# The sequence transform of an FNet layer as seven products of block sums, with an accumulating DMA

## The chip, the cores and the metric

One Trainium2 chip, one NeuronCore. The metric is the device time of one execution in microseconds (us), the median of the runs shown. PE is the matmul engine, DVE the vector engine, ACT the scalar engine, POOL is GpSimd, and SP is the engine whose queue issues nearly all DMAs here.

## The reference

Two independent halves, each 2048 x 1024, end up side by side in one output of 2048 x 2048 in float32.

```python
# left half: sliding-window attention, 32 heads of 32, window 256
q, k, v = split_heads(x @ wqkv)
scores  = where(0 <= i - j < 256, (q @ k.T) * 32 ** -0.5, -1e9)
a       = concat_heads(softmax(scores) @ v) @ wo
# right half: FNet mixing, only the real part
re = x @ dft_hid_re.T;  im = x @ dft_hid_im.T            # "first spectral product"
y  = dft_seq_re @ re - dft_seq_im @ im                   # "second spectral product", 2048 x 2048 by 2048 x 1024
out = concatenate([a, y], axis=-1)
```

## The kernel before

Every float32 operand is scaled by a power of two found from its own largest value, and split into a high and a low float16 part; a product is three matmul passes (high x high, high x low, low x high: `PASSES`). One matmul is 128 x 128 weights by 128 x 512 moving columns.

The program runs in this order on PE. First the projections q, k and v (`order`, 96 products of 24 matmuls). Then the spectral half, `units`: for each part p (0 is the real part, 1 the imaginary part) 16 units "x" and then 16 units "c". An x unit i multiplies the 128 rows i of x by the hidden DFT matrix, two column halves e of 24 matmuls each, and ACT and DVE write the result as a high and a low half into `ain` (a view of the large tile `reg1`). A c unit i multiplies 128 rows of the cosine (or sine) matrix by all 16 row blocks in `ain`: two halves e of 48 matmuls each. For p = 0 ACT copies each half from PSUM into a tile `y` (line 764), which goes to a DRAM scratch `y1s`; for p = 1 `y` is loaded back from there, DVE adds the new product (line 766), and `y` goes to `out`. Last comes the output projection "po" of the attention (line 792), which already works with seven products of block sums instead of eight blocks.

The rows of a unit are fetched two units ahead (`u_load`), scaled and split one unit ahead (`u_split`; the splits run in `split`, lines 109 to 112, ACT writing the high part and DVE the low part; on the page DVE's part has line 106). For a c unit the largest absolute value of its 128 x 2048 rows is found by two DVE reductions (`u_top`, tile `top_u`), spread over the partitions by a PE transpose, and turned into a scale (`scale_of`).

The attention is a generator (`attention`) of 256 blocks, cut into two steps each. `tick` pulls `rate` steps for each matmul of the main work, so the blocks are spread evenly under the projections and the spectral half; it must be done before the last c units (`LAST`), where `wo_blocks` prepares the weights of the output projection. One block is: scores on PE (line 212), a masked copy, a maximum and a bias on DVE (220, 222, 225), two exponentials and a float16 copy on ACT (228, 231), the low part on DVE (232), a DMA transpose, two mask selections on POOL (245, 247), and the weighted sum of v on PE (274), closed by three small DVE operations (280, 282, 285) per two blocks and a split of `o` per eight blocks (294, 295).

The order of instructions on each engine is not that of the code: the framework's scheduler sets it at build time from its own estimates. Each engine then runs its queue strictly in that order and waits at the head of it. PSUM holds three banks for the main products (`ps_m`, tags m0 to m2, used in turn through `bank`), two pairs of banks for the scores, and one for the sums of v.

## Time and profile before

| | us |
|---|---|
| median of 3 runs | 1841.79 (1839.05 to 1841.85) |
| the profiled execution's own time | 1839.44 |
| its span, first to last instruction | 1837.7 |
| projections, up to the first x unit | 571 |
| x units, p = 0 and p = 1 | 571 to 764, 1133 to 1328 |
| c units, p = 0 and p = 1 | 764 to 1133, 1328 to 1686 |
| output projection | 1686 to 1837 |

The page gives each engine's busy time; the stage bounds above are the first and last starts of the groups of each stage. The granted PE clock is 0.997 over the span. A group's mean duration counts the overlap of neighbours: a matmul row of 379 ns follows its neighbour after less than that, so the pace of PE is read from runs of matmuls in the timeline, not from the mean.

### The profile page before, as it was taken

The numbers are of one execution on the slowest core, as the hardware profiler recorded it, in microseconds if no ns is written. First come the engines' busy times: TensorE is split into PE (matmuls) and PEld (weight loads), VectorE is DVE, ScalarE is ACT, GpSimd is POOL, SyncE is SP. The second block draws the span as 40 slices with busy tenths as digits, with TensorE's granted clock in tenths as the row PEclk, the third lists the DMA queues.
The fourth block names the chain that finished last, engine by engine and source line by source line (L and its number), as shares of the span: only waits on it lengthen the run. The fifth ranks groups of instructions, "written<-read, shape, count | busy, mean of one in ns | idle before, by whom it ended". The sixth has DMA issues, their size and how long they took to land.

```text
span 1837.7 us, 29866 instructions
## 1 busy us (share of the span) xinstructions
PE 1820.5 (99%) x11260; PEld 892.2 (49%) x11260; DVE 1233.2 (67%) x2444; ACT 755.1 (41%) x1207; POOL 327.5 (18%) x489
## 2 busy tenths in 40 slices
PE   7999999999999999999999999999999999999998
PEld 3444455445544554555455544554554455444443
DVE  7665887786666665777776666666677676685451
ACT  3332443454444444454444444544443333332221
POOL 0000122212212221222122212221222122200000
PEclk9999999999999999999999999999999999999999
DMA  5357799997676655568776676665486666662331
GB/s 229 115 181 207 212 221 233 233 218 167 153 171 146 127 127 117 133 171 183 173 151 153 155 155 166 127 138 121 95 198 173 162 161 146 146 184 69 115 104 69
DMA packets 438288, 289.55 MB, mean 158 GB/s; under 512 B 338816, under 2 KB 396160, under 8 KB 438144
## 3 DMA queue, kind: packets, MB, share of 16 engines
q1 hardware_dynamic: 438144, 287.65, 63.5%
q8 instruction: 88, 1.44, 0.3%
q14 instruction: 56, 0.46, 0.1%
HBM read 155.32 MB, written 58.85 MB: 117 GB/s over the span
## 4 chain that ended last, share of the span: by engine, by line
PE 94%; DVE 3%; DMA 1%; ACT 1%; issue 1%; SPq 0%; ACTq 0%; DVEq 0%
PE p L338 51%; PE pk L338 9%; PE pv L338 9%; PE po L792 8%; PE pq L338 8%; PE s L212 4%; PE pv L274 4%; DVE reg L106 1%; DMA raw_x<-in_xa_dram 0%; DVE raw_wo L664 0%; ACT reg L111 0%; DVE top_x L106 0%; DMA raw_wd<-in_wd_dram 0%; DVE ext L106 0%; DVE un L106 0%
## 5 line engine op out<-in xcount | busy, mean ns | idle before, releaser
L338 PE MATMUL p<-reg,un 128*128 128x512 f16 x4608 | 1048.1, 379 | 1.1 <-DVE un L106 1.0
L338 PEld LDWEIGHTS <-un 128*128 128x128 f16 x4608 | 439.8, 97 | 492.7 <-DVE un L106 2.0
L228 ACT ACTIVATE s<-s,bias,esc 128x256 f32<-128x256 f32 (+1 forms) x512 | 268.6, 528 | 554.8 <-DVE bias L225 454.5
L245 POOL TENSOR_SCALAR_AFFINE_SELECT z<-t 128x512 f16<-128x512 f16 x224 | 158.6, 708 | 1041.2 <-DMA t<-hl 946.0
L232 DVE TENSOR_TENSOR hl<-s,hl 128x512 f16<-128x512 f32 (+1 forms) x256 | 170.7, 670 | 195.5 <-ACT hl L231 194.7
L338 PE MATMUL pq<-reg,wu_q 128*128 128x512 f16 x768 | 176.1, 385 | 6.7 <-ACT reg L111 4.3
L338 PE MATMUL pk<-reg,wu_k 128*128 128x512 f16 x768 | 174.4, 379 | 0.0
L338 PE MATMUL pv<-reg,reg 128*128 128x512 f16 x768 | 172.9, 379 | 0.0
L222 DVE TENSOR_REDUCE mx<-s 128x2 f32<-128x512 f32 (+1 forms) x256 | 170.5, 667 | 3.1
L247 POOL TENSOR_SCALAR_AFFINE_SELECT t<-t 128x512 f16<-128x512 f16 x224 | 163.9, 732 | 15.3
L231 ACT ACTIVATE hl<-s 128x512 f16<-128x512 f32 (+1 forms) x256 | 148.4, 584 | 6.7
L212 PE MATMUL s<-qk,qk 96*128 96x128 f16 (+2 forms) x704 | 147.8, 275 | 0.0
L220 DVE COPY_PREDICATED s<-upper,s 128x256 f32<-128x256 uint32 x224 | 94.4, 423 | 63.4 <-PE s L212 61.8
L338 PEld LDWEIGHTS <-wu_q 128*128 128x128 f16 x768 | 74.9, 99 | 95.9 <-issue 12.1
L338 PEld LDWEIGHTS <-reg 128*128 128x128 f16 x768 | 73.7, 98 | 83.8
L338 PEld LDWEIGHTS <-wu_k 128*128 128x128 f16 x768 | 73.6, 98 | 82.3
L106 DVE SCALAR_TENSOR_TENSOR un<-raw_u,sc_u,un 128x1024 f16<-128x1024 f32 x64 | 86.7, 1383 | 23.2 <-ACT un L111 22.9
L274 PE MATMUL pv<-vt,t 128*128 128x65 f16 x1984 | 99.3, 185 | 0.0
L212 PEld LDWEIGHTS <-qk 96*128 96x128 f16 x704 | 65.8, 98 | 66.9
L274 PEld LDWEIGHTS <-t 128*128 128x128 f16 x1984 | 89.2, 96 | 10.9 <-POOL t L247 0.3
L111 ACT ACTIVATE un<-raw_u,sc_u 128x1024 f16<-128x1024 f32 x64 | 69.9, 1140 | 46.5 <-DVE sc_u L106 46.5
L274 PE MATMUL pv<-vt,z 128*128 128x65 f16 (+1 forms) x896 | 88.4, 185 | 0.0
(138 smaller groups left out, 1472.3 us busy)
## 6 DMA issues: line engine op xcount, KB each, us to landing
raw_u<-in_cs_dram SPq DMA_DIRECT2D x64, 512.0 KB, 4.9
qk<-qs SPq DMA_DIRECT2D x192, 128.0 KB, 3.2
raw_u<-in_xb_dram SPq DMA_DIRECT2D x32, 512.0 KB, 4.0
vs<-yv SPq DMA_DIRECT2D x32, 260.0 KB, 2.8
vt<-vs SPq DMA_DIRECT2D x32, 260.0 KB, 3.9
raw_x<-in_xa_dram SPq DMA_DIRECT2D x16, 512.0 KB, 10.2
qs<-yq SPq DMA_DIRECT2D x32, 256.0 KB, 2.4
raw_scan<-in_xb_dram SPq DMA_DIRECT2D x16, 512.0 KB, 4.2
```

Of the source, the lines that this page charges most:

```text
L106: latest[:] = [f(*args, **kwargs)]
L212: nc.tensor.matmul(s[:, j, at:at + (k1 - k0) * P], q2s[g, sc][:, h, i * P:i * P + P], k2s[g, k0 // QB][:, h, k0 % QB * P:k0 % QB * P + (k1 ...
L220: nc.vector.copy_predicated(s[:, :, 2 * P:3 * P], upper2, s[:, :, :P] if nb == 3 else never2)
L222: nc.vector.tensor_reduce(mx, sv, axis=AX.X, op=ALU.max, negate=True)
L228: nc.scalar.activation(sv[:, h], sv[:, h], AF.Exp, bias=bias[:, h:h + 1], scale=es)
L231: nc.scalar.activation(hi, sv, AF.Copy)
L232: behind[:] = [nc.vector.tensor_tensor(lo, sv, hi, op=ALU.subtract)]
L245: nc.gpsimd.affine_select(out=z, in_=pk, compare_op=ALU.is_gt, fill=0.0, base=0, pattern=[[0, 4], [-1, P]], channel_multiplier=1)
L247: nc.gpsimd.affine_select(out=pk, in_=pk, compare_op=ALU.is_ge, fill=0.0, base=0, pattern=[[0, 4], [1, P]], channel_multiplier=-1)
L274: nc.tensor.matmul(pvt[:, r, j, lo:], weights(part, j, kb), vts[g, k // QB][:, k % QB, at + lo:at + VW], start=(m == 0), stop=(m == len(se ...
L338: nc.tensor.matmul(ps, lhs(hl, d), rhs(hr, d), start=(m == 0), stop=(m == 3 * n - 1))
L792: nc.tensor.matmul(ps, lhs[pos](hl, k), slot(pos)[:, hr, k], start=(m == 0 and fresh), stop=(m == 11), skip_group_check=True)
```

## The change

The second spectral product is cut into four rounds: for each part p, two halves c of the contraction (1024 of 2048 rows). A round is 8 x units and then 8 c units. The x units of a round go in the order 0, 4, 1, 5, 2, 6, 3, 7, so that after each pair the two blocks to be combined are there: ACT evacuates them in float32 to a tile `tb` (line 828), and `t_blocks` forms from each pair seven block sums, high and low, in `tsum` (in `reg1`, where `ain` was): four subtractions, on POOL for the first three pairs and on DVE for the last, and copies on ACT and DVE.

A c unit now covers two row tiles (256 output rows) and half the contraction. `u_split` scales its two raw tiles, forms four sums of blocks on POOL in place (lines 631 and 640, 128 x 512 each), and splits seven 128 x 512 blocks in the tiles un_a, un_b, un_c and a spare part of `reg1`. `seven` then runs seven products of 12 matmuls (positions 0, 3, 2, 1, 4, 5, 6) into three PSUM banks: positions 0, 2, 4 and 6 go one after the other into bank a, 1 and 5 into bank b, 3 into bank c. Two positions after the first go on accumulating in a bank that has been read in between, so the read must be over before the next product starts there. Bank a of one unit is bank b of the next. ACT copies positions 0, 2, 1 and 6 to `y`, DVE adds 3, 4 and 5 there (lines 857 and 855).

There are three `y` buffers, two for each unit: the first of a unit, finished by position 6, is the second of the next unit, first written by that unit's position 2 or 1. In the first round SP stores them plainly to `out`; in the other three POOL issues a DMA that adds them to `out` in DRAM (line 864, 48 transfers of 512 KB). `y1s` is gone, with its 16 stores and 16 loads.

Moved besides: the search for the scale of a c unit goes from DVE to ACT, which sums absolute values (line 606, 64 passes over 128 x 1024); the factor `fc`, the scaling of `o` by the softmax sums and the low part of `ohl` go from DVE to POOL; raw tiles are fetched three units ahead; `rate` rises from 0.0869 to 0.0922 steps for each matmul, and the last-but-one c unit of the last round is now where the attention must be done.

```diff
-            nc.vector.tensor_tensor(                       # scaling of o, 128 times
+            nc.gpsimd.tensor_tensor(
-            nc.vector.tensor_tensor(ohl[:, 1], o, ohl[:, 0], op=ALU.subtract)
+            nc.gpsimd.tensor_tensor(ohl[:, 1], o, ohl[:, 0], op=ALU.subtract)
...
-    MM_ATT = 24 * (len(order) - START) + 4 * NT * 24 + 4 * NT * 48
+    MM_ATT = 24 * (len(order) - START) + 4 * 8 * 48 + 4 * 8 * 84
...
     for p in range(2):
-        units += [("x", p, i) for i in range(NT)] + [("c", p, i) for i in range(NT)]
+        for c in range(2):
+            units += [("x", p, c, 4 * (i % 2) + i // 2) for i in range(8)] + [("c", p, c, q) for q in range(8)]
...
     def u_top(n):
-            for k in range(2):
-                top(f"u{n}", raws[n][k], k, 2)
+            for j in range(2):
+                with tc.issue_after(behind_act[0].ins) if behind_act else nullcontext():
+                    nc.scalar.activation(junk, raws[n][j].rearrange("p d t -> p (d t)"), AF.Abs,
+                                         scale=2.0 ** -10, accum_out=tops[key][:, j:j + 1])
...
     def u_split(n):
+        nc.gpsimd.tensor_scalar(fc[n], fa[:, p:p + 1], v[:, 0:1], None, op0=ALU.mult)
+        ua, uc, ub = (stp.tile([P, 2, ND, P], F16, tag="st", name=f"un{n}_{k}") for k in "acb")
+        split(ua[:, 0], ua[:, 1], r1, s)
+        split(ud[:, 0], ud[:, 1], r2[:, 4:], s)
+        gsub(r1[:, :4], r1[:, :4], r2[:, :4])
+        nc.gpsimd.tensor_tensor(r2[:, :4], r2[:, :4], r2[:, 4:], op=ALU.add)
+        gsub(r2[:, 4:], r2[:, 4:], r1[:, :4])
+        gsub(r1[:, 4:], r1[:, 4:], r2[:, 4:])
+        return [lambda: split(uc[:, 0], uc[:, 1], r2, s), lambda: split(ub[:, 0], ub[:, 1], r1, s)]
...
+    def t_blocks(k, a, b):
+        def fill(i, src):
+            hi = tsum[:, i:i + 2, 0, k]
+            nc.scalar.activation(hi, src, AF.Copy)
+            nc.vector.tensor_tensor(tsum[:, i:i + 2, 1, k], src, hi, op=ALU.subtract)
+        sub = gsub if k < 3 else (lambda o, x, y: nc.vector.tensor_tensor(o, x, y, op=ALU.subtract))
+        nc.scalar.activation(tsum[:, 0, 0, k], a[:, 0], AF.Copy)
+        nc.vector.tensor_tensor(tsum[:, 0, 1, k], a[:, 0], tsum[:, 0, 0, k], op=ALU.subtract)
+        fill(1, b)
+        sub(a[:, 1], a[:, 1], a[:, 0])
+        sub(b[:, 1], b[:, 1], a[:, 1])
+        sub(a[:, 0], b[:, 1], a[:, 0])
+        sub(b[:, 0], b[:, 0], b[:, 1])
+        fill(5, b)
+        fill(3, a)
...
+    def seven(name, q, lhs, rhs, done):
+        banks = {}
+        for pos in (0, 3, 2, 1, 4, 5, 6):
+            role = "abacaba"[pos]
+            fresh = pos in (0, 1, 3)
+            if fresh:
+                tag = {"a": q % 2, "b": 1 - q % 2, "c": 2}[role]
+                banks[role] = ps_m.tile([P, CH], F32, tag=f"m{tag}", name=f"{name}_{pos}")
+            ps = banks[role]
+            m = 0
+            for k in range(4):
+                for hl, hr in PASSES:
+                    nc.tensor.matmul(ps, lhs[pos](hl, k), rhs(pos)[:, hr, k], start=(m == 0 and fresh),
+                                     stop=(m == 11), skip_group_check=True)
...
-                    product(ps, lambda h, k: c2[k // 8][:, h, k % 8], lambda h, k: ain[:, k, h, e], NT)
+            y1, y2 = ybufs[ny[0] % 3], ybufs[(ny[0] + 1) % 3]
+            ny[0] += 2
+            def done(pos, ps):
+                y = {0: y1[:, 0], 3: y1[:, 0], 2: y2[:, 0], 1: y2[:, 1], 4: y2[:, 1], 5: y2[:, 0], 6: y1[:, 1]}[pos]
+                if pos in (3, 4, 5):
+                    behind[:] = [nc.vector.scalar_tensor_tensor(y, ps, f, y, op0=ALU.mult, op1=ALU.add)]
+                else:
+                    behind_act[:] = [nc.scalar.activation(y, ps, AF.Copy, scale=f)]
+                if pos in (5, 6):
+                    if p == 0 and c == 0:
+                        nc.sync.dma_start(dst, src)
                     else:
+                        nc.gpsimd.dma_start(dst, src, accum_op=ALU.add)
```

The first place is ACT in the c units. In the rows, `y_20` or `y0` is the output tile, `p2_20_0` the PSUM bank of a product of unit 20, `s_` and `hl_` the scores and their float16 copy, `un` the split weights, `junk` the output nobody reads of the search. Before, in unit 20 of p = 0, the copies of two products stand two blocks of attention apart:

```order
L764 ACTIVATE y_20_9453<-p2_20_0_9454,fc20_9150 128x512
L228 ACTIVATE s_126_9542<-s_126_9542,bias_126_9564,esc_3_2482 128x256 x2
L231 ACTIVATE hl_126_9568<-s_126_9542 128x512
L228 ACTIVATE s_127_9593<-s_127_9593,bias_127_9615,esc_3_2482 128x256 x2
L231 ACTIVATE hl_127_9619<-s_127_9593 128x512
L764 ACTIVATE y_20_9453<-p2_20_1_9577,fc20_9150 128x512
```

After, at the border of units 28 and 29 (second round), ACT has:

```order
L111 ACTIVATE un30_a_12127<-raw_u30_0_11584,sc_u30_12118 128x1024
L111 ACTIVATE reg1_81<-raw_u30_1_11586,sc_u30_12118 128x512
L857 ACTIVATE y0_6318<-p2_28_0_11871,fc28_11571 128x512
L229 ACTIVATE s_165_12149<-s_165_12149,bias_165_12163,escs_109 128x256
L111 ACTIVATE reg2_82<-raw_wd1_1_2_12142,vwd_100 128x1024
L229 ACTIVATE s_165_12149<-s_165_12149,bias_165_12163,escs_109 128x256
L232 ACTIVATE hl_165_12167<-s_165_12149 128x512
L857 ACTIVATE y0_6318<-p2_29_0_12144,fc29_11850 128x512
L606 ACTIVATE junk_6317,top_u31_12242<-raw_u31_0_11863 128x1024
L857 ACTIVATE y0_6318<-p2_29_1_12249,fc29_11850 128x512
```

The copy of unit 28's position 6 and that of unit 29's position 2 now stand four instructions apart and write the same buffer `y0`; between them the buffer must have gone to DRAM.

The second place is POOL. Before, at the same attention blocks, it has only mask selections (`z`, `t`):

```order
L245 AFFINE_SELECT z_159_11957<-t_159_11735 128x512
L247 AFFINE_SELECT t_159_11735<-t_159_11735 128x4x128
L245 AFFINE_SELECT z_162_12132<-t_162_11955 128x512
L247 AFFINE_SELECT t_162_11955<-t_162_11955 128x4x128
L245 AFFINE_SELECT z_163_12214<-t_163_11997 128x512
```

After, the selections share its queue with the sums of the raw cosine tiles, the scaling of `o`, and the adding DMAs:

```order
L864 DMA out_0_dram<-y1_6319 128x1024
L246 AFFINE_SELECT z_163_12238<-t_163_12020 128x512
L248 AFFINE_SELECT t_163_12020<-t_163_12020 128x4x128
L624 TENSOR_SCALAR fc30_12125<-fa_102,sc_u30_12118 128x1
L286 TENSOR_TENSOR o_5_0_12176<-os_160_12191,rs_160_12189 128x2x64
L864 DMA out_0_dram<-y0_6318 128x1024
L640 TENSOR_TENSOR raw_u30_0_11584<-raw_u30_0_11584,raw_u30_1_11586 128x512
L631 TENSOR_TENSOR raw_u30_1_11586<-raw_u30_1_11586 128x512
L640 TENSOR_TENSOR raw_u30_1_11586<-raw_u30_1_11586,raw_u30_0_11584 128x512
L286 TENSOR_TENSOR o_5_0_12176<-os_162_12313,rs_162_12311 128x2x64
```

The second DMA row sends unit 28's `y0`; it waits for ACT's copy, and the sums for unit 30 stand behind it.

The third place is PE at the same border. Before, a c unit is two runs of 48 matmuls, each into another bank, with the attention's matmuls in between. The border of the two runs of unit 20, with a score matmul at it:

```order
L338 MATMUL p2_20_0_9454<-reg1_82,un20_1_9155 128x512
L212 LDWEIGHTS qk0_3_3_8901
L212 MATMUL s_126_9542<-qk1_3_3_8897,qk0_3_3_8901 128x384
L338 LDWEIGHTS un20_0_9152
L338 MATMUL p2_20_1_9577<-reg1_82,un20_0_9152 128x512
```

After, runs of twelve alternate between banks; here the first row of each run of main products, from unit 28's position 6 (un28_b) over unit 29's positions 2, 1, 4, 5 and 6, with position 3 of unit 30 drawn forward:

```order
L793 MATMUL p2_28_0_11871<-reg1_81,un28_b_11575 128x512
...
L793 MATMUL p2_29_0_12144<-reg1_81,un29_c_11853 128x512
...
L793 MATMUL p2_29_1_12249<-reg1_81,un29_b_11854 128x512
...
L793 MATMUL p2_30_3_12411<-reg1_81,un30_a_12127 128x512
...
L793 MATMUL p2_29_0_12144<-reg1_81,un29_c_11853 128x512
...
L793 MATMUL p2_29_1_12249<-reg1_81 128x512
...
L793 MATMUL p2_29_0_12144<-reg1_81,un29_b_11854 128x512
```

Each run of twelve into p2_29_0 must wait until the bank has been read after the run before it; between two of them lie one or two runs of twelve and the attention's matmuls.

More of the change, by code (lines that the diff above doesn't have):

```diff
@@ L13 @@
 BF16 = mybir.dt.bfloat16
-U16 = mybir.dt.uint16
+U8 = mybir.dt.uint8
 U32 = mybir.dt.uint32
@@ L440, in scores_scale @@
     def scores_scale(g):
-        e1 = const.tile([P, 1], F32, name=f"e1_{g}")
-        e = esc[g] = const.tile([P, NCH], F32, name=f"esc_{g}")
+        e1 = small.tile([P, 1], F32, tag="top0", name=f"e1_{g}")
+        e = esc[g] = escs[:, g]
         nc.vector.tensor_scalar(e1, vw["k", g][:, 0:1], vX[:, 0:1], SCALE * UP * UP, op0=ALU.mult, op1=ALU.mult)
@@ L609, in fused_kernel @@
     at(len(order) - 2, u_load, 1)
+    at(len(order) - 1, u_load, 2)
     with tc.tile_pool(name="pa", bufs=2) as pa:
@@ new lines, in fused_kernel @@
+                    behind_act[:] = [nc.scalar.activation(tb[:, e], ps, AF.Copy, scale=tf[:, p, e:e + 1])]
+                    if rest:
+                        rest.pop(0)()
+                pair.append(tb)
+                if len(pair) == 2:
+                    t_blocks(i % 4, *pair)
+                    pair = []
+                continue
+            if p == 1 and c == 1:
+                if i == LAST:
+                    while agen[0] is not None:
+                        if next(agen[0], 0) == 0:
+                            agen[0] = None
+                    att_cm.__exit__(None, None, None)
+                    late = ctx.enter_context(tc.tile_pool(name="late", bufs=8, side="right"))
+                    ext = late.tile([P, 3, 2, 4, CH], F16, tag="ext", bufs=1, name="ext")
+                    wo_blocks(late, 0)
+                if i == LAST + 1:
+                    wo_blocks(late, 1)
@@ L774, in fused_kernel @@
+            seven(f"p2_{n}", i, uns.pop(n), lambda pos: tsum[:, TPOS[pos]], done)
+            if p == 1 and c == 1 and i == 6:
+                o_load(0)
+                o_load(1)
+                o_blocks(late, 0)
         copy = lambda y, ps: nc.scalar.activation(y, ps, AF.Copy, scale=fo)
         add = lambda y, ps: nc.vector.scalar_tensor_tensor(y, ps, fo, y, op0=ALU.mult, op1=ALU.add)
-        banks = {}
         for q in range(NT // 2):
@@ L780, in fused_kernel, with done @@
             y1, y2 = (late.tile([P, 2, CH], F32, tag="raw", name=f"yo{q}_{k}") for k in range(2))
[L781 to L796 removed]
+            def done(pos, ps):
+                y = {0: y1[:, 0], 3: y1[:, 0], 2: y2[:, 0], 1: y2[:, 1], 4: y2[:, 1], 5: y2[:, 0], 6: y1[:, 1]}[pos]
+                (add if pos in (3, 4, 5) else copy)(y, ps)
                 if pos >= 5:
```

166 lines of the change are left out of this document (79 added, 87 removed).

## The prediction

> **What bounds the kernel now.** I read the page's busy times first, then the chain, then the stages.
>
> ```profile
> PE 1820.5 (99%) x11260; PEld 892.2 (49%) x11260; DVE 1233.2 (67%) x2444; ACT 755.1 (41%) x1207; POOL 327.5 (18%) x489
> PE 94%; DVE 3%; DMA 1%; ACT 1%; issue 1%; SPq 0%; ACTq 0%; DVEq 0%
> ```
>
> PE is busy for all but 17 us of the 1837.7, and the chain that ended last is PE for 94%. So a matmul less is time less, as long as the others keep up. The stages (windows of x, c, x and c units; columns are busy us and instructions of each engine, PE clock, DMA share, GB/s):
>
> ```profile
> 571.00:764.00 193.00, 193.00 (x1275) 96.36 (x1274) 125.62 (x252) 91.36 (x155) 42.26 (x60) 1.00 0.55 121
> 764.00:1133.00 369.00, 369.00 (x2453) 185.52 (x2451) 254.19 (x544) 173.67 (x279) 87.03 (x117) 1.00 0.72 164
> 1328.00:1686.00 358.00, 356.94 (x2245) 175.69 (x2244) 255.44 (x499) 129.79 (x198) 65.62 (x91) 1.00 0.62 157
> ```
>
> In the first c window PE has no idle time at all, at the full clock, while DVE is at 69%, ACT at 47%, POOL at 24% and DMA at 72%. That is the stage that changes.
>
> **What the removed matmuls are worth.** The pace of PE stands in a run of the timeline, and in the same 4 us what I fear below:
>
> ```profile
> 941.75 3.62 PE L338 MATMUL p<-reg,un 128*128 128x512 f16 x16
> 945.31 2.11 PE L338 MATMUL p<-reg,un 128*128 128x512 f16 x9
> 945.09 0.60 ACT L231 ACTIVATE hl<-s 128x512 f16<-128x512 f32 x1
> 947.36 1.11 ACT L228 ACTIVATE s<-s,bias,esc 128x256 f32<-128x256 f32 x2 [1.68 <-DVE bias L225]
> 948.40 0.68 ACT L764 ACTIVATE y<-p,fc 128x512 f32<-128x512 f32 x1
> ```
>
> Sixteen matmuls take 3.62 us, the last ends 0.379 after its start (the group's mean), so one takes (3.62 - 0.379) / 15 = 0.216 us. A c unit had 2 x 48 = 96 and has 7 x 12 = 84; over 32 units 384 are gone: 384 x 0.216 = 82.9 us. The x units keep theirs. A c unit lasted 369 / 16 = 23.06 us, of which 96 x 0.216 = 20.74 its own and 2.33 attention. The new one has 18.14 of its own and 2.33 x (84 x 0.0922) / (96 x 0.0869) = 2.16 of attention: 20.3 us. Against that every other cost is set.
>
> **Do the other engines still fit under 20.3 us?** The prices, by form:
>
> ```profile
> L106 DVE SCALAR_TENSOR_TENSOR un<-raw_u,sc_u,un 128x1024 f16<-128x1024 f32 x64 | 86.7, 1383 | 23.2 <-ACT un L111 22.9
> L106 DVE TENSOR_REDUCE top_u<-raw_u 128x1 f32<-128x1024 f32 x64 | 74.8, 1208 | 0.0
> L111 ACT ACTIVATE un<-raw_u,sc_u 128x1024 f16<-128x1024 f32 x64 | 69.9, 1140 | 46.5 <-DVE sc_u L106 46.5
> L735 DVE SCALAR_TENSOR_TENSOR reg<-p,reg 128x512 f16<-128x512 f32 x64 | 44.0, 688 | 26.0 <-ACT reg L734 25.4
> L285 DVE TENSOR_TENSOR o<-os,rs 128x128 f32<-128x128 f32 x128 | 40.1, 314 | 0.3
> L734 ACT ACTIVATE reg<-p 128x512 f16<-128x512 f32 x64 | 38.0, 594 | 44.3 <-PE p L338 43.6
> L766 DVE SCALAR_TENSOR_TENSOR y<-p,fc,y 128x512 f32<-128x512 f32 x32 | 23.9, 748 | 30.4 <-PE p L338 30.3
> L295 DVE TENSOR_TENSOR ohl<-o,ohl 128x512 f16<-128x512 f32 x32 | 22.6, 706 | 17.7 <-ACT ohl L294 17.6
> L764 ACT ACTIVATE y<-p,fc 128x512 f32<-128x512 f32 x32 | 21.8, 683 | 11.2 <-PE p L338 11.1
> L106 DVE SCALAR_TENSOR_TENSOR reg<-raw_wd,vwd,reg 128x1024 f16<-128x1024 f32 x16 | 20.6, 1289 | 16.9 <-ACT reg L111 16.9
> L664 DVE TENSOR_TENSOR uo<-r,uo 128x1024 f16<-128x1024 f32 x16 | 19.5, 1221 | 28.0 <-ACT uo L714 28.0
> L714 ACT ACTIVATE uo<-r 128x1024 f16<-128x1024 f32 x16 | 16.7, 1051 | 58.7 <-PE po L792 41.3 <-PE p L338 17.5
> L664 DVE TENSOR_TENSOR r<-r,r 128x512 f32<-128x512 f32 x24 | 16.5, 688 | 0.5
> L245 POOL TENSOR_SCALAR_AFFINE_SELECT z<-t 128x512 f16<-128x512 f16 x224 | 158.6, 708 | 1041.2 <-DMA t<-hl 946.0
> ```
>
> ACT in a c unit: 173.67 / 16 = 10.85 us. Out go two splits (2 x 1.14), two copies (2 x 0.683) and half a wd split (0.57); 6.63 is left, and 6.15 at 0.928 of the attention. In come splits of 3.5 tiles (3 x 1.14 + 0.6), four copies (2.73), and the search, two passes over 128 x 1024 (its own price is in no row; between 1.05 of line 714 and 1.38 of the slowest pass of that size; I take the 1.14 of the same engine and input: 2.28). Sum 15.2 of 20.3, 75%.
>
> DVE: 254.19 / 16 = 15.9. Out: two splits (2.77), two searches (2.42), `fc` and half a wd split (0.9), two scalings of `o` and half an `ohl` (1.0); 8.8 left, of which about 1.2 finds scales and 7.6 is attention, so 8.3. In: splits 3 x 1.383 + 0.75, three adds at 0.748: 15.4, 76% where it was 69%.
>
> POOL: 5.44 x 0.928 = 5.05, and four sums of 128 x 512. No row has POOL doing a sum of two tensors; the bounds are a selection of that size (0.71) and one that was held up (1.68, below). I take 1.1, nearer the free one since it reads two inputs: 4.4. With two scalings, half an `ohl`, `fc` (together 1.6 at the same doubt) and two DMA issues of about 1 each, 13 of 20.3 us, 64%. The Trainium skill, GPSIMD Engine Reference, section 3.1, gives 4497 ns for a sum over 2048 float32, an estimate of 1.12 us here; by it the sum is the same within 0.1 us a unit.
>
> An x unit is 10.4 of its own and about 1.8 of attention: 12.2 us. DVE had 125.62 / 16 = 7.85; two low halves (1.38) become half of `t_blocks` ((0.688 + 3 x 1.221) / 2 = 2.2) and a share of its four subtractions in the last pair (0.3), with `o` and `ohl` off: 8.5. ACT goes from 5.7 to 5.7 - 1.19 + 1.37 + 1.87 = 7.8. Both fit.
>
> So no engine becomes the bound by its sum. The search, the splits, the sums, `y1s` (32 transfers that hid under a saturated PE) cost or give nothing by themselves; the cover is PE, and it leaves 5 us a unit on ACT and DVE. What can cost is order.
>
> **The term for late reads.** The old product left a bank alone for two more runs. The new one wants bank a back after one run of twelve (2.6 us) and about 0.3 of attention. Take off the read itself (0.7): a read may start 2.2 us after its product's end.
>
> ```profile
> ACT y L764: 11.1, 10
> DVE y L766: 30.3, 18
> PE po L792 <- DVE yo L775: 0.7, 1, 0.7
> PE po L792 <- ACT yo L774: 0.6, 1, 0.6
> ```
>
> The first two rows (who waited for the tile p: us, times) say that of 32 copies on ACT 10, and of 32 adds on DVE 18, found their engine idle; the rest came to a queue. I set the end of each run of 48 in the timeline against the start of its read: the mean delay is 0.9 on ACT and 1.0 us on DVE. Four of 32 on ACT exceed 2.2 us, by 2.7 us together; five of 32 on DVE, by 10.8, four of them after 1620 where `wo_blocks` is also on DVE. The rows quoted above are one of the four: the run ended at 945.15, ACT stood at an exponential until DVE's bias came, and the copy began at 948.40, 3.25 us late. Nobody waited then. With four binding copies and two binding adds a unit, 128 and 64 in all, this is 4 x 2.7 + 2 x 10.8 = 32 us, and with ACT at 75 / 47 and DVE at 76 / 69 of their old loads 41: the upper end. The lower end is the output projection, where seven products already run with the same single run of slack, though without attention: 1.3 us for 56 products (last two rows), 5 for 224. I take 25, nearer the c stage since the attention is what makes reads late, but below 32 since the DVE delays at 1620 come once and not in each round.
>
> **The term for the borders.** After the last x pair of a round the chain is copy 0.68, fill 1.05 + 1.22, three subtractions 2.06, fill 2.27: 7.3 us, with another 2.3 for the third fill. PE's queue has there twelve matmuls of position 0 and 27 with k below 3 that need nothing of that pair: 39 x 0.216 = 8.4 us. Cost 0 to 3 us a round; I take 1, 4 in all.
>
> **The adding DMA.**
>
> ```profile
> y1s<-y SPq DMA_DIRECT2D x16, 512.0 KB, 3.1
> y<-y1s SPq DMA_DIRECT2D x16, 512.0 KB, 3.6
> out_dram<-y SPq DMA_DIRECT2D x16, 512.0 KB, 2.9
> ```
>
> These are medians from issue to landing. No row has a transfer that adds. It cannot beat the plain store of the same tile (2.9); the other end is a load and a store one after the other, 6.7. I take 4.8. Its slack: the `y` buffer that position 6 fills is written again by position 2 of the next unit. In PE's order that is one run of twelve later (2.9 us with attention), and two more runs (5.8) pass before PE wants the bank of that read: 8.7 less two copies with their 0.25 delay (1.9) is 6.8 us from issue to landing, POOL's own delay included. The row of DMAs waits at the head of POOL's queue for ACT; behind it stand the sums of the unit after next and the mask selections, which PE's v sums wait for. They have time:
>
> ```profile
> POOL z L245 <- DMA t<-hl: 260.0, 53, 19.1
> 902.92 2.86 DVE L106 SCALAR_TENSOR_TENSOR un<-raw_u,sc_u,un 128x1024 f16<-128x1024 f32 x2 [1.66 <-ACT un L111]
> 903.02 1.68 POOL L245 TENSOR_SCALAR_AFFINE_SELECT z<-t 128x512 f16<-128x512 f16 x1 [5.82 <-DMA t<-hl]
> 904.77 1.50 POOL L247 TENSOR_SCALAR_AFFINE_SELECT t<-t 128x512 f16<-128x512 f16 x1
> ```
>
> In the c window POOL waited 260 of 369 us for transposes. With one operation ahead of it (0.7) the DMA lands at 5.5: no stall. At the upper end, 6.7 and 1.7 ahead, 8.4, it is 1.6 us late in each of 24 units: 38 us. Likeliest 0.
>
> The last three rows are a lock: beside two DVE splits from SBUF, each at its usual length, POOL's selections took 1.68 and 1.50 instead of 0.71. The Trainium skill (SBUF — State Buffer, section "SBUF: two separate sides", and "A bandwidth-pool intuition that's wrong" below it) calls the port pair of DVE and GpSimd an exclusive lock, and says that a DMA whose descriptors GpSimd writes then starves, 620 ns becoming about 3100. The rows agree on the lock; no run here shows the starving. By it an estimated 2.5 us come on top, 8.0 us, and 1.2 x 24 = 29 us of the gain are lost.
>
> **Sum.** -82.9 + 25 + 4 + 0 = -54. The profiled execution took 1839.4 (span 1837.7), so 1785.5; the median of the runs is 2.4 above it, so I say 1787.
>
> **Rivals.**
> - Clean: the scheduler's order hides the reads as in the output projection. -82.9 + 5 + 0 = -78: 1764. For it: PE's 100% and the single-run slack of "po". Against: there the attention is over.
> - Queues fill: 41 for reads and 12 at borders, or 25 and the DMA's upper end: -30 to -16, 1812 to 1826. For it: ACT from 47% to 75%, and exponentials that stop it; POOL's lock. Against: the delays over 2.2 us are few.
> - Slower: the adding DMA lands late. Past 6.8 us each us costs 24; at 6.8 + 54 / 24 = 9.1 us from issue the gain is gone, at 11 it is 1787 + 4.2 x 24 = 1888. ACT would stand at the copy of position 2 or 1, with the exponentials behind it. For it: DMA is already 72% busy, the adding transfers double their traffic, and no row prices them. Against: both ends from the rows are below 9.1.
> - No difference: the terms at their upper ends cancel 83.
>
> **How the numbers follow.** Likeliest (1770 to 1805) 0.45, clean (below 1770) 0.13, queues (1805 to 1838) 0.18, none (within 0.2%, 3.7 us, about what a measurement tells from no change) 0.04, slower 0.20. Faster: 0.76. The range goes from 1757, PE's bare 82.9, to 1855, a DMA at 9.7 us; it leaves out some 0.04 below and 0.12 above.
>
> **What would show it.** After: PE at 97% or more in c units of about 21 us, its waits on the copies and adds of lines 857 and 855 some 25 us in sum, on `tsum` a few; no copy on ACT ended by an out DMA; out DMAs from POOL landing in 4 to 6 us; POOL sums at 1.1 us; DVE and ACT at three quarters. Wrong if ACT's copies wait for the DMA queue, if POOL sums take 2 us, or if the splits of un_b and un_c come later than their products.

## The result, and the profile after

The changed kernel is slower: 1943.7 us median (1936.5 to 1946.4, four runs) against 1840.4 beside it, a ratio of 1.056 [1.053, 1.059]. Predicted were 1787, and a slower kernel had a chance of 0.20. The profiled execution took 1936.5 (span 1934.8). First the busy times and the chain of the page:

```profile
PE 1789.8 (93%) x10876; PEld 864.3 (45%) x10876; DVE 1289.2 (67%) x2338; ACT 984.4 (51%) x1559; POOL 739.2 (38%) x905
PE 55%; DMA 12%; DVE 10%; ACT 8%; issue 7%; POOL 7%; SPq 0%; POOLq 0%; ACTq 0%; DVEq 0%
```

The matmuls went as said, 11260 to 10876. PE's idle time did not stay at 17 us: it is 1934.8 - 1789.8 = 145. And 384 matmuls less at 0.216 should have left 1820.5 - 82.9 = 1737.6 us of busy PE; there are 52 us more, for which no instruction was added (they are taken up below, with the clock). In the chain DMA went from 1% to 12%, ACT from 1% to 8%, and POOL stands in it at 7%.

The windows by stage (as before: us, busy and instructions by engine, clock, DMA share, GB/s), one x stage and the four c stages:

```profile
580.00:675.00 95.00, 94.56 (x653) 47.89 (x652) 62.54 (x114) 58.57 (x95) 53.69 (x59) 1.00 0.62 141
675.00:860.00 185.00, 169.31 (x1089) 82.67 (x1090) 130.82 (x254) 115.59 (x190) 100.50 (x110) 0.97 0.62 153
965.00:1178.00 213.00, 172.99 (x1049) 82.23 (x1048) 139.98 (x254) 123.62 (x195) 104.16 (x119) 0.92 0.78 153
1286.00:1490.00 204.00, 175.72 (x1106) 85.43 (x1105) 135.17 (x255) 118.28 (x194) 105.31 (x126) 0.93 0.73 142
1588.00:1790.00 202.00, 171.94 (x945) 78.95 (x944) 142.03 (x211) 109.00 (x156) 96.53 (x99) 0.93 0.63 131
```

The x stage shown is full. A c stage of eight units should take 8 x 20.3 = 162 us; the first, which stores plainly from SP, takes 185, and the three that add take 213, 204 and 202. No engine is near full in any of them: DVE 66 to 71%, ACT 54 to 62%, POOL 48 to 54%. So the loss is in waits. The two waits of ACT on an earlier output (us, times, longest; the third `y` buffer lies in `reg1` and is named reg), and then PE's four largest:

```profile
ACT y L857 <- DMA out_dram<-y: 56.7, 16, 7.3
ACT reg L857 <- DMA out_dram<-reg: 36.1, 7, 8.4
```

```profile
PE s L213 <- DVE hl L233: 29.4, 21, 4.0
PE p L793 <- ACT y L857: 26.2, 15, 7.4
PE p L793 <- ACT reg L857: 20.4, 8, 7.3
PE p L793 <- ACT tb L828: 11.1, 2, 5.9
```

ACT's copies waited 93 us for an earlier output to land, 23 times. The longest such stall of PE in the timeline, with what followed:

```profile
1011.22 0.67 ACT L857 ACTIVATE y<-p,fc 128x512 f32<-128x512 f32 x1
1012.19 0.90 POOL L864 DMA_DIRECT2D out_dram<-y  x1 [1.91 <-ACT y L857]
1024.30 0.69 ACT L857 ACTIVATE y<-p,fc 128x512 f32<-128x512 f32 x1 [6.91 <-DMA out_dram<-y]
1025.04 4.34 PE L793 MATMUL p<-reg,un_c 128*128 128x512 f16 x12 [7.40 <-ACT y L857]
```

The copy of position 6 ends at 1011.9, POOL issues the adding DMA at 1012.2, and the next copy into that buffer starts at 1024.3: it stood 6.9 us, PE 7.4. This transfer took 12 us to land, far more than the median below: the landings scatter. Then twelve matmuls take 4.34 us. More runs of twelve, by the time PE was idle ahead of them (in brackets):

```profile
1729.49 2.75 PE L793 MATMUL p<-reg,un_c 128*128 128x512 f16 x12 [2.19 <-ACT reg L857]
1404.52 4.04 PE L793 MATMUL p<-reg 128*128 128x512 f16 x12 [2.79 <-ACT reg L857]
1433.08 5.11 PE L793 MATMUL p<-reg,un_c 128*128 128x512 f16 x12 [5.70 <-ACT y L857]
1075.22 4.84 PE L793 MATMUL p<-reg,un_c 128*128 128x512 f16 x12 [7.28 <-ACT reg L857]
1079.90 2.32 PE L793 MATMUL p<-reg,un_a 128*128 128x512 f16 x10
```

2.75 us is the full pace. In these rows it holds after 2.2 us of idle; after 2.8 and more the run is 1.3 to 2.4 us longer, and the next shown is at full pace again (ten in 2.32). So a stall is paid a second time, by the clock: its mean over the span is 0.968, where it was 0.997. In the stretches whose granted clock is 0.50 PE is busy for 89 us in all, and before for 8; half of the difference, some 40 of the 52 us, is what the halved clock costs. For the rest there is an estimate only: PE's work is broken 76 times more often (92 waits over 0.15 us against 16), and the last matmul of a run counts 0.379 us where one with a neighbour counts 0.216, which makes 12. The Trainium skill, "TensorE: Matmul & The Clock Gate", Part 1 (The HAM clock gate) and its section "HAM oscillation — how this bites in real kernels", states the rule: half the clock after an idle window of about 3.4 us, and as long to come back. The rows agree with the halving (5.11 us against 2.75) and the return; here 2.79 us of idle was already enough, and a row further down shows 2.32.

The adding DMAs, with the plain stores of the first round beside them (median us to landing; then the packets, MB and share of the 16 engines' span of POOL's queue), and groups of POOL and ACT:

```profile
out_dram<-y POOLq DMA_DIRECT2D x32, 512.0 KB, 7.0
out_dram<-reg POOLq DMA_DIRECT2D x16, 512.0 KB, 7.3
out_dram<-y SPq DMA_DIRECT2D x11, 512.0 KB, 4.0
q0 software_dynamic: 6912, 25.17, 7.8%
```

```profile
L640 POOL TENSOR_TENSOR raw_u<-raw_u,raw_u 128x512 f32<-128x512 f32 x96 | 132.7, 1382 | 23.0 <-DVE un_a L106 20.5
L631 POOL TENSOR_TENSOR raw_u<-raw_u 128x512 f32<-128x512 f32 x32 | 42.2, 1318 | 1.2
L286 POOL TENSOR_TENSOR o<-os,rs 128x128 f32<-128x128 f32 x128 | 69.2, 540 | 72.7 <-DVE os L283 72.5
L606 ACT ACTIVATE junk<-raw_u 128x1024 uint8<-128x1024 f32 x64 | 67.5, 1054 | 0.2
```

An adding DMA lands after 7.0 to 7.3 us (medians) where 4.8 were taken, above the slack of 6.8. A sum on POOL takes 1.38 or 1.32 us where 1.1 was taken, 132.7 + 42.2 = 175 us in all, and a scaling of `o` 0.54. A pass of the search (last row, ACT) takes 1.05, less than the 1.14 taken.

### The profile page after: what moved, and what is told of

Its sections match the earlier page's. It is cut to its first block, busy times and chain, and to the rows that moved or that the text cites. A ratio compares the mean times of both kernels' runs of the same rounds, so it can differ in the third digit from the quotient of the medians.

```text
span 1934.8 us, 29981 instructions
## 1 busy us (share of the span) xinstructions
PE 1789.8 (93%) x10876; PEld 864.3 (45%) x10876; DVE 1289.2 (67%) x2338; ACT 984.4 (51%) x1559; POOL 739.2 (38%) x905
## 4 chain that ended last, share of the span: by engine, by line
PE 55%; DMA 12%; DVE 10%; ACT 8%; issue 7%; POOL 7%; SPq 0%; POOLq 0%; ACTq 0%; DVEq 0%
PE p L339 12%; PE pk L339 9%; PE p L793 8%; PE po L793 7%; PE pq L339 7%; PE pv L339 7%; DMA t<-hl 5%; DMA out_dram<-y 3%; PE s L213 3%; POOL raw_u L640 2%; PE pv L275 2%; DMA raw_wd<-in_wd_dram 2%; ACT s L229 1%; DMA out_dram<-reg 1%; ACT junk L606 1%
## 5 line engine op out<-in xcount | busy, mean ns | idle before, releaser
L229 ACT ACTIVATE s<-s,bias,escs 128x256 f32<-128x256 f32 (+1 forms) x512 | 266.4, 529 | 319.5 <-DVE bias L226 274.0
L339 PE MATMUL p<-reg,un 128*128 128x512 f16 x1536 | 349.4, 380 | 0.0
L793 PE MATMUL p<-reg,un_c 128*128 128x512 f16 x768 | 196.8, 403 | 38.6 <-ACT y L857 18.4
L339 PEld LDWEIGHTS <-un 128*128 128x128 f16 x1536 | 146.8, 98 | 164.3 <-issue 1.5
L793 PE MATMUL p<-reg,un_a 128*128 128x512 f16 x768 | 188.8, 389 | 23.1 <-ACT tb L828 11.1
L793 PE MATMUL p<-reg,un_b 128*128 128x512 f16 x768 | 184.1, 386 | 12.1 <-DVE reg L855 3.6
L640 POOL TENSOR_TENSOR raw_u<-raw_u,raw_u 128x512 f32<-128x512 f32 x96 | 132.7, 1382 | 23.0 <-DVE un_a L106 20.5
L793 PEld LDWEIGHTS <-un_c 128*128 128x128 f16 x768 | 77.1, 102 | 131.0 <-issue 50.6
L793 PEld LDWEIGHTS <-un_a 128*128 128x128 f16 x768 | 74.6, 99 | 112.1 <-issue 22.4
L793 PEld LDWEIGHTS <-un_b 128*128 128x128 f16 x768 | 74.7, 99 | 97.1 <-issue 19.1
```

Of the source, the lines that this page charges most:

```text
L229: nc.scalar.activation(sv[:, h], sv[:, h], AF.Exp, bias=bias[:, h:h + 1], scale=es)
L339: nc.tensor.matmul(ps, lhs(hl, d), rhs(hr, d), start=(m == 0), stop=(m == 3 * n - 1))
L640: nc.gpsimd.tensor_tensor(o, a, b, op=ALU.subtract)
L793: nc.tensor.matmul(ps, lhs[pos](hl, k), rhs(pos)[:, hr, k], start=(m == 0 and fresh), stop=(m == 11), skip_group_check=True)
```

## The experiments

Theories: A, the adding DMA lands late and holds the `y` buffers; B, the border between rounds (copies of `tb` behind splits, and the ring of raw tiles); C, POOL's sums; D, the queues of ACT (D1) or DVE (D2), with short waits at the banks. E and F came later: the adding DMA costs POOL's queue (E), or costs by the adding itself (F). Times are medians, ratios to the kernel before.

### Where the output goes

**Plain stores** (1881.6 us, 1.022 [1.019, 1.024]). All rounds store as the first does, so the accumulation over the rounds is left out:

```
-                    if p == 0 and c == 0:
-                        nc.sync.dma_start(dst, src)
-                    else:
-                        nc.gpsimd.dma_start(dst, src, accum_op=ALU.add)
+                    nc.sync.dma_start(dst, src)
```

> Every round writes its part of y to the output with the plain store from SP that the first round uses, so the second to fourth round overwrite instead of adding: the accumulation over rounds is left out, all else stays. Theory A (the adding DMA lands late, and with three y buffers PE's p banks wait for the copies): the three later c stages (213, 204 and 202 us) fall to the 185 us of the first, that is 28 + 19 + 17 = 64 us, and the time goes to about 1880 us; ACT's y and reg copies no longer wait for a DMA. Theory B (the border between two rounds and the raw tile ring): within 10 us of the changed kernel, 1935 to 1945 us. Theory C (the load of ACT, DVE and POOL, with POOL's sums of 1.38 us): within 15 us, since only 48 issues of 0.9 us leave POOL.

A's number, to 2 us: the output costs 62 of the 104 us lost. But one of A's signs failed: ACT's copies still waited 37 us for an output. So the landing was not all of it.

**Halves** (1920.5, 1.044 [1.042, 1.045]). Each half of `y` is sent when its last product is in it.

> The accumulation stays; each half of y is sent as soon as its last product is in it, as 96 transfers of 256 KB in place of 48 of 512 KB on POOL's queue and as many halves from SP in the first round. Theory A: a half is free some 5 us earlier than the whole was, and its landing should be shorter than the 7.0 to 7.3 us of the whole, so most of the 93 us of ACT's waits for a landing goes; 30 to 60 us gained, 1885 to 1915 us. Theory B: no change, 1935 to 1945. Theory C: 48 more issues of 0.9 us on POOL, 43 us more of it, some of which shows as later sums: 1945 to 1970 us.

A gain of 23 us, under A's 30 to 60 though ACT's waits fell from 93 to 43.

**Ring of halves** (1915.4, 1.041 [1.039, 1.044]). All six halves in one ring:

```
-            y1, y2 = ybufs[ny[0] % 3], ybufs[(ny[0] + 1) % 3]
+            ya, yb, yc, yd = (ybufs[(ny[0] + k) % 6] for k in range(4))
...
-                y = {0: y1[:, 0], 3: y1[:, 0], 2: y2[:, 0], 1: y2[:, 1], 4: y2[:, 1], 5: y2[:, 0], 6: y1[:, 1]}[pos]
+                y = {0: ya, 3: ya, 2: yb, 5: yb, 1: yc, 4: yc, 6: yd}[pos]
```

> The accumulation stays, all of the product is computed. The six halves of the three y buffers form a ring that is taken in the order in which a unit's halves are first written, and each half is sent as soon as its last product is in it. The place of a half is written again 7 products of 12 matmuls after its last product at the earliest, some 20 us, where a whole buffer gave 6.8 us of room. Theory A (the adding DMA lands late): ACT waits for an output DMA for under 5 us in all (93 us in the changed kernel), and the time is that with plain stores, 1882 us, within 8. Rival (the adding DMAs cost by what they take from others: POOL's 96 issues of 0.94 us, their reads of the output, the other transfers): the waits go and the time doesn't come below 1900 us.

No copy on ACT waits for a landing any more, and only 28 us come back. A is a part; 34 us of the output's 62 remain, as the rival said. The 28 are a net figure: 96 issues stand on POOL now where 48 stood, and PE's waits moved. First the changed kernel, then the ring, then the kernel with plain stores from POOL (below):

```profile
PE pv L275 <- POOL z L246: 6.1, 2, 4.8
```

```profile
PE pv L275 <- POOL z L246: 19.9, 6, 6.6
```

```profile
PE pv L275 <- POOL z L246: 6.9, 4, 2.6
```

PE's waits for ACT's copies of `y` fell from 26.2 + 20.4 to 10.4 + 3.5 us with the ring, and its waits for POOL's selections `z` rose by 14.

**Delayed issue** (1919.9, 1.043 [1.041, 1.045]). The issue is written three products later in the code.

> As the kernel with the ring of halves, but each adding DMA is issued on POOL three products (some 8 us) after the product that ends its half, so that POOL needn't stand at the issue until the last add or copy is done; all is computed. Theory E (with the ring no buffer is late any more, and the 34 us that remain over the plain stores are POOL's queue: it stood 106 us at the issues, with attention's selects and the block sums behind it): POOL's waits at the issues fall below 20 us, PE's waits for z and t (24 us) and ACT's for the sums (66 us) fall, and the time is 1880 to 1890 us. Rival (the adding DMA's reads and writes take memory and queues from other transfers): 1905 to 1915 us, no change.

This told nothing of E: the scheduler put the instructions of every engine in the same order as for the ring. It is a repetition of that program, 4.5 us away from it (four runs each, 1913.5 to 1923.0 and 1917.2 to 1922.4), and so a measure of what two builds of one order can differ by.

**Pinned issue** (1913.7, 1.041 [1.039, 1.043]). With `fc` on DVE (below), and each issue tied behind a later select on POOL, which did change POOL's order:

```
+                with tc.issue_after(last_pool[0].ins):
                     nc.gpsimd.dma_start(dst, y, accum_op=ALU.add)
```

> As the kernel with fc on DVE (1907.5 us), but each adding DMA stands on POOL behind the last select of attention that was written down three products after the product that ends its half; the kernel called delay had kept the same order on POOL as the ring, so it told nothing. Theory E: POOL's wait at the issues falls from 95 us to under 50, and 10 to 20 us are gained, 1888 to 1898 us. Rival F, or the 0.9 us of each issue alone: within 5 us of 1907.5.

6 us above its base, not 10 to 20 below. But POOL's wait at the issues of `y` fell only from 95 to 71 us, where E's test wanted under 50; the next run says more of E.

**Plain stores from POOL** (1883.4, 1.024 [1.022, 1.025]). The ring, in the same order on all engines, with only `accum_op` gone:

```
-                        nc.gpsimd.dma_start(dst, y, accum_op=ALU.add)
+                        nc.gpsimd.dma_start(dst, y)
```

> As the kernel with the ring of halves, in the same order of instructions on POOL and ACT, but POOL's 96 DMAs write plainly and do not add (the accumulation over rounds is left out). It tells the adding from the issuing. Theory E (POOL's queue stands at the issue until the last add or copy is done, and each issue takes 0.94 us): the adding itself costs nothing once no buffer is late, and the time stays at 1915 to 1920 us, as the ring's. Rival F (the adding takes memory and DMA time from the other transfers): it falls to the plain stores' 1882 us, or most of the way.

F: 32 us go with the adding alone. The time is within 2 us of the plain stores from SP, but those have whole buffers, and 37 us of ACT's waits for an output, which the ring has not; so what 96 issues from POOL cost by themselves isn't shown. The rows of the DMAs (queue, then landing), of the ring and then of the plain stores from POOL:

```profile
q0 software_dynamic: 13824, 25.17, 9.4%
out_dram<-y POOLq DMA_DIRECT2D x64, 256.0 KB, 5.5
```

```profile
q0 software_dynamic: 7680, 25.17, 3.8%
out_dram<-y POOLq DMA_DIRECT2D x64, 256.0 KB, 3.7
```

The groups of issues on POOL, the ring's and then the plain stores':

```profile
L865 POOL DMA_DIRECT2D out_dram<-y x64 | 58.2, 923 | 81.0 <-DVE y L856 53.0 <-ACT y L858 20.4 <-DVE sc_u L106 4.0
```

```profile
L865 POOL DMA_DIRECT2D out_dram<-y x64 | 36.9, 576 | 86.0 <-DVE y L856 57.1 <-ACT y L858 22.9 <-DVE sc_u L106 4.3
```

For the same bytes an adding transfer takes 2.5 times the DMA engines' time, 1.8 us longer to land, and 0.35 us more of POOL at each issue. POOL waits at the issue for as long in both (81.0 and 86.0), and yet 32 us go: the standing at the issue is not their cause, and E falls. How the 32 us divide between DMA time and POOL's 96 x 0.35 = 33 us was not taken apart; a sign for POOL's part is that PE's waits for `z` fall by 13 us, from 19.9 to 6.9 (rows above).

### The border

**Two units ahead** (1956.7, 1.063 [1.060, 1.065]) and **both** (1873.8, 1.018 [1.015, 1.022]), the second with plain stores too:

```
-            u_load(n + 3)
+            u_load(n + 2)
```

> The raw tiles are fetched two units ahead in place of three, so the last x unit's tb copies find a free raw buffer and needn't wait for the splits of the first c unit. Theory B: the four borders lose 7 to 14 us of idle PE each and the low clock behind it, some 45 us together: about 1900 us, and the windows at the borders show PE at 26 of 28 us and a clock near 1. Theory A: nothing at the borders comes from the output, and the c stages stay at 202 to 213 us: within 10 us of 1944. Rival to both: two units ahead is too short for the fetch, and the x stages (95 to 108 us) grow; then it is slower than 1944 us.

> Both edits together: plain stores from SP in all rounds (accumulation left out), and raw tiles two units ahead. If A and B are separate causes, their gains add: 64 + 45 = 109 us, about 1835 us. If one stall hides behind the other, it is no better than the better of the two alone (about 1880). What is left above the 1787 us predicted would be theory C (load of ACT, DVE and POOL) and the first round's c stage, 185 us where 162 were predicted, in all four rounds: 4 x 23 = 92 us, of which some 45 are the border's.

B's 1900 is missed on the wrong side by 57 us; with the adding DMA in place shorter fetching costs 13, without it it gains 8. The gains do not add to 109. The rival's sign is there: ACT's splits in the x stages wait 31 us for the raw tile's load, where they waited 5.

**Copies first** (1913.8, 1.040 [1.037, 1.042]):

> As the kernel with the splits two products later and the raw tiles two units ahead (1908.9 us), but at the four borders ACT copies both halves of the last tb before it splits un_c and un_b of the first c unit. Theory B: the four borders lose 7 to 10 us of idle PE each, of which half is this order: 15 to 25 us faster, 1884 to 1894 us. Rival: un_c is then late for the third product by as much as tb was for the first, and it stays within 5 us of 1909.

No change: 4.8 us above its base, the kernel with splits later and tiles two units ahead (below). The first border in the windows, of that base and of this kernel:

```profile
666.00:696.00 30.00, 22.70 (x157) 11.32 (x155) 24.33 (x47) 18.67 (x29) 18.27 (x19) 0.87 0.50 124
```

```profile
666.00:696.00 30.00, 25.09 (x172) 11.86 (x170) 25.50 (x51) 19.53 (x31) 21.14 (x19) 0.94 0.54 143
```

PE's idle time at it went from 7.3 to 4.9 us, and at all four such borders from 27.8 to 22.5. So the order of the copies is 5 of those 28 us, too little to be seen in the total. B, as it was put, falls.

### Sums, search and pace

**No sums**, on the ring (1870.0, 1.016 [1.014, 1.019]), and **plain stores and no sums** (1838.2, 0.999 [0.998, 1.000]): the four lines of sums in `u_split` are left out, so the product is another one.

> As the kernel with the ring of halves, but the four block sums of each c unit on POOL are left out: un_c and un_b are split from the raw tiles as they come, so the product is another one; every split, matmul and transfer stays. Theory C (POOL's sums of 1.38 us, on the way to un_c and un_b and against DVE's reads of the same memory): 40 to 60 us faster than the ring of halves, some 1825 to 1840 us. Theory D (what is left are many short waits for copies in ACT's and DVE's queues, each with one product of room in its bank, and the low clock after the longer of them): POOL is not on that path; 0 to 15 us faster, 1865 to 1882 us.

> Plain stores from SP in all rounds (no accumulation) and no block sums on POOL, so the product is another one; three whole y buffers, all splits, matmuls and transfers stay. If the output DMA (62 us) and the sums (45 us) are separate terms, they add: 1944 - 62 - 45 = 1837 us. If both are one queue's load (POOL's), the second gives less once the first is gone: 1850 to 1870 us. What stays over the 1787 us predicted is then in neither: borders, short waits at the banks, the low clock.

45 us on the ring and 43 beside plain stores: the sums are a term of their own, and with the output they add as expected (1838 for 1837). In the ring kernel these were ACT's waits for them, 66 us; in the changed kernel, where ACT also stood for landings, they were 27:

```profile
ACT un_c L111 <- POOL raw_u L640: 54.0, 24, 8.1
ACT un_b L111 <- POOL raw_u L640: 12.3, 14, 2.6
```

ACT stands at a split that needs a sum, with the copies that PE needs behind it. That this is the way by which the sums cost is read from the rows; no run takes these waits away and leaves the sums.

**Splits later** (1911.7, 1.038 [1.036, 1.041]), with and without the shorter fetching (1908.9, 1.038 [1.035, 1.040]), and **fc on DVE** (1907.6, 1.037 [1.035, 1.039]), on which they build:

```
-                if pos in (3, 4) and rest:
+                if pos in (1, 5) and rest:
```

> As the kernel with the delayed issue, but the factor fc of a c unit, one product of two columns that waits for the unit's scale, goes from POOL back to DVE, where the scale is made. Theory E (POOL's queue): POOL stood 46 to 81 us at fc, of which most is ahead of the unit's sums, which wait for the same scale in any case: 5 to 15 us faster than the delayed issue alone. Rival: the sums wait for the split un_a after it anyway, 0 to 3 us.

> As the kernel with fc on DVE, but un_c and un_b of the next unit are split two products and one product later in a c unit (after the products 1 and 5 in place of 3 and 4). Theory C (POOL's sums are late and ACT stands at the split that needs them, with the copies of y behind it: 54 and 12 us in the ring kernel): ACT's wait for raw_u goes below 20 us, 10 to 20 us faster. Rival (the splits are then late for the next unit's third product, or the raw tiles are free too late for the loads): slower by 5 to 20 us.

> As the last, with the raw tiles fetched two units ahead. From the pair of kernels with plain stores (7.8 us between their medians) 0 to 10 us faster than the last; if the raw tiles come late, since un_b is now read later and a load is only issued at the unit's start, up to 15 us slower.

fc gives 8 us over the ring and 12 over its repetition, little beside the 4.5 between those two. The later splits give nothing; they were to bring ACT's wait for the sums below 20 us, but it stayed at 59 (58 before), so they don't test it. 1907.6 is the lowest of all that compute the whole product, 67 us above the kernel before.

**Pace** (1948.7, 1.058 [1.056, 1.060]) and **search on DVE** (1933.8, 1.051 [1.049, 1.053]), each on the ring:

```
-                        tick(4)
+                        tick(4 * WC)
```

> As the kernel with the ring of halves, but the attention's steps are spread otherwise over the matmuls: 0.75 of the present rate in the c units, 1.19 of it in the projections and the x units, the same number in all. Theory D (load and order of ACT and DVE in the c stages set the waits): the c stages, some 180 us each, lose a third to a half of their 20 us of waits, and the x stages don't grow by as much: 20 to 40 us faster, 1840 to 1860 us. Rival: the projections and x units have no room either (DVE 71% busy there), and it is the same or slower, 1880 to 1900 us.

> As the kernel with the ring of halves, but the search over the cosines goes back to DVE: two TENSOR_REDUCE of 1.21 us for a c unit there in place of two passes of 1.05 us and two reads of 0.19 us on ACT. Theory D1 (ACT's queue is the late one: y, reg and tb copies wait in it): 10 to 25 us faster, 1857 to 1872 us. Theory D2 (DVE's queue is the late one: hl, un, adds): 10 to 25 us slower, 1892 to 1907 us. Theory C: no change, within 5 us.

The pace is the rival's and worse: 33 us lost, so the earlier stages have no room. The first x unit starts at 626 us where it started at 579, and all behind it is only 11 us shorter. The search costs 18 us more on DVE than on ACT.

**No search** (1811.2, 0.984 [0.983, 0.986]) and **o on DVE** (1840.7, 1.001 [1.000, 1.003]), each on plain stores without sums (1838.2):

> As the kernel with plain stores and no block sums (1838 us), and the search over the cosines is left out as well: the scale of a c unit comes from a constant that DVE writes, so ACT does 80 us less. If the search in ACT's queue makes the copies late (D1), 15 to 30 us faster, 1808 to 1823 us. If DVE is the late engine (D2, as moving the search there by itself cost 16 us), 0 to 8 us faster.

> As the kernel with plain stores and no block sums (1838 us), and attention's o and ohl go back from POOL to DVE: 128 operations of 0.31 us and 32 of 0.71 us there (before's rows) in place of 0.54 and 1.2 us on POOL. If the way over POOL makes attention late (ACT waits some 35 us for o, PE for z), 5 to 15 us faster, 1823 to 1833 us. If DVE is the late engine (D2), 5 to 15 us slower.

Without the search, whose scale is then a constant, 27 us go, D1's number. Its way back to DVE had cost 18 us on the ring. `o` and `ohl` may stand on either engine. The busy times without sums, then without the search as well:

```profile
PE 1766.7 (96%) x10876; PEld 860.4 (47%) x10876; DVE 1265.7 (69%) x2338; ACT 981.2 (54%) x1559; POOL 533.4 (29%) x729
```

```profile
PE 1752.5 (97%) x10876; PEld 856.6 (47%) x10876; DVE 1258.9 (70%) x2370; ACT 914.8 (51%) x1431; POOL 532.4 (29%) x729
```

PE's busy time for the same 10876 matmuls falls with the waits: 1789.8, 1766.7, 1752.5. How long an idle time slows the clock is not fixed. Two rows of the first of these kernels, and one of the second:

```profile
1661.55 2.75 PE L789 MATMUL p<-reg,un_b 128*128 128x512 f16 x12 [2.69 <-DVE y L851]
1640.14 5.28 PE L789 MATMUL p<-reg,un_b 128*128 128x512 f16 x12 [3.11 <-DVE reg L851]
1602.55 4.44 PE L786 MATMUL p<-reg,un_c 128*128 128x512 f16 x12 [2.32 <-ACT y L850]
```

Twelve matmuls keep the full pace after 2.69 us of idle in one place, and take 4.44 us after 2.32 in another.

## Why the prediction was wrong

What the runs take off 1944, step by step: 28 (buffers held by late landings, ring), 32 (adding, plain from POOL), 2 (to whole buffers and plain from SP, within the noise), 43 (sums), 27 (search): 1811. Each figure holds the clock's share in it, and goes by this order of the steps.

- **The removed matmuls**: right in count; their 83 us are what is left to gain when nothing else waits. With the output plain and sums and search left out, 29 of them show.
- **The adding DMA**, "Likeliest 0": the step that failed most, 62 us. The landing was mis-sized, 7.0 to 7.3 us where 4.8 was taken; both bounds, 2.9 and 6.7, were below it. Put into the text's own rule, 7.2 and 0.7 of POOL's delay are 1.1 us past 6.8, 24 times: 26 us, and the ring gave 28. That they meet is luck: the rule takes one landing for all, but landings scatter (12 us in the row above), PE stood behind ACT's copies of `y` 23 times, for 2.0 us on average and up to 7.4, the clock fell behind the longer stalls, and the ring's 28 is net of what it adds on POOL. The other 32 us are no late buffer: they go when the adding goes, with its DMA time and POOL time, for which the sum had no term. The rival "Slower" had named the waits at the copies; it set no price for this half either. The Trainium skill's rule on starved descriptors (SBUF — State Buffer, "A bandwidth-pool intuition that's wrong") gave an estimated 29 us of loss, near the 28 too; but its cause isn't what is seen: the same queue, storing plainly beside the same DVE work, lands 256 KB in 3.7 us.
- **Do the other engines still fit**: the loads a unit are near the forecast. In the first c stage ACT has 115.59 / 8 = 14.4 us (15.2 were said), DVE 16.4 (15.4), POOL 12.6 (13), and no engine is full. The conclusion from it, that search and sums "cost or give nothing by themselves", failed: 43 to 45 us for the sums and 27 for the search. The sums were mis-sized by a quarter (1.38 for 1.1), but within the bounds named; what was missing, as far as the rows show, is that ACT waits in order for a sum, and PE for what stands behind ACT.
- **The late reads**, 25 us: about right. In plain stores from SP, PE waited 9.9 + 8.0 + 6.8 + 6.7 = 31 us for copies and adds, some of them late for an output; in plain stores from POOL, where no copy waits for an output, it was 6.6 + 2.1 + 9.2 + 7.3 = 25. The rows of the first:

```profile
PE p L793 <- ACT y L857: 9.9, 10, 2.4
PE p L793 <- ACT reg L857: 8.0, 7, 2.7
PE p L793 <- DVE y L855: 6.8, 5, 1.9
PE p L793 <- DVE reg L855: 6.7, 3, 3.3
```

- **The borders**, 4 us: too small. In the changed kernel's window of the first border PE is idle for 8.7 us:

```profile
672.00:700.00 28.00, 19.29 (x139) 8.72 (x138) 22.42 (x47) 19.64 (x33) 9.73 (x12) 0.88 0.43 95
```

  But no run turned a shorter border into a shorter kernel, so its price in the total is open.
- **The clock** had no term. The span is 1934.8 - (1837.7 - 82.9) = 180 us above one without any new cost; 128 of these are PE's idle time, 52 its longer busy time for the same matmuls, of which some 40 are the halved clock.

Open: the 24 us between 1811 and 1787, the price of the borders, how F divides, and by which waits the sums and the search cost.

## What to carry to other kernels

A kernel whose PE is 99% busy is not one whose other engines are free: with 50 to 70% on in-order queues that wait for one another, new work on any of them can be paid for though busy shares leave room: 80 us of search cost 27, 175 of sums 43. Price an output that adds above a plain store (here 1.5 times in landing, 2.5 in DMA time, 1.6 in issue), and give its buffer slack for the late landings, not for the median; a ring in the order of first use costs no memory. And charge a long stall of PE twice, once for the wait and once for the slow matmuls behind it (1.3 to 2.4 us here after 2.8 us and more).

## What was not expected of the hardware

- An adding transfer of 512 KB lands in 7.0 to 7.3 us, one of 256 KB in 5.5, a plain one of 256 KB from the same queue in 3.7. Its issue holds POOL 0.92 us, the plain one's 0.58.
- No fixed idle time sets the clock's fall in the rows read: twelve matmuls took 2.75 us after 2.69 of idle, 4.04 after 2.79, and 4.44 after 2.32.
- Two builds with the same order of instructions on every engine differed by 4.5 us in their medians of four runs.
